# Attention in front of two MoE layers: where in two passes the next pair of heads' bias is read

## The chip, the cores and the metric

The kernel runs on one NeuronCore of one Trainium2 chip. The metric is the device time of one launch in microseconds. Three runs of the kernel before took 1263.3, 1264.17 and 1265.56 us; the median is 1264.17 us. The change and every reading of the trace here are about that one core.

## The reference

The program is an attention layer followed by a dense MoE layer and a second MoE layer whose gate is balanced by row and column sums. Only the attention matters for the change:

```python
B, H, S, D = 2, 8, 576, 64
scores = scale * np.matmul(q, k.transpose(0, 1, 3, 2))
psi_rel = np.log1p(np.abs(rel))
x = (psi_rel / psi_i)[..., None]
h = np.maximum(x @ w1 + b1, 0.0)
bias = h @ w2
scores = scores + bias.transpose(2, 0, 1)[None, :, :, :]
attn = np.exp(scores - max); attn = attn / (sum + 1e-09)
out = np.matmul(attn, v)
...
```

The bias belongs to a head and a pair of positions, and not to a batch: both batches add the same bias.

## The kernel before, in words

The kernel has three stages. First `bias_emit` builds the bias of all heads and writes it to five tensors in HBM, `wt0` to `wt4`, one for each of the five blocks of query rows (four of 128 rows, one of 64). Then `attention` (L350) runs. Last come the two MoE layers, set up in `experts` and started by `rest`.

Heads go in pairs, so there are four pairs, and each pair has two passes, one per batch: pass i works on pair i // 2 and on batch i % 2. A pass has nine steps, one for each of `TILES` (L57), which names the block of query rows t and the head o of the pair. Block 1 and block 0 come first, then 3, 4 and 2. The step number r within a pass places all side work by hand, and s = 9 i + r counts the steps over all eight passes. `soft` (L377, its instruction is at L386) adds the bias to the scores in PSUM on DVE and takes the minimum; ACT then takes the exponential, POOL or ACT the division, PE the transposes and the product with v.

The side work that the prediction follows:

- `read(hp, t)` (L1136) reads block t of pair hp's bias from HBM into a tile that has two buffers, so pair hp + 1 writes the buffer that pair hp - 1 has left. Blocks 0 to 3 are one DMA each (L1147). Block 4 is three DMAs (L1149 to L1151). All are issued on SyncE's queue (SP).
- `load` (L296) brings q (`qr`, L306), k (`kr`, L306) or v (L300) of a pass to SBUF, q and k as two DMAs each. q and k share one buffer, `raw`, so k of a pass can only be loaded when q of that pass has been used up, and q of the pass after that only when k has.
- `prep(i, k)` (L308) cuts q and k into a high and a low part: DVE copies the high part (L282, `qh` or `ks`), POOL subtracts (L321 `ql`, L332 `ks`). By `PREPS` (L59), pass i's steps 0 and 4 do this for pass i + 1: at step 0 the parts of q, and behind them the load of k for pass i + 1; at step 4 the parts of k, and behind them the load of q for pass i + 2. `VLOAD` puts the load of v at step 2.
- `beside` (L993) places early work of the MoE by `EARLY` (L72). Six of its weight loads (L581) stand at s = 10, 12, 30, 34, 42 and 48, and DVE and POOL convert the loaded weights in four parts; the first part of the first piece (L590, DVE) stands at s = 14, which is step 5 of pass 1.

What sets the order: SP issues its DMAs strictly in the order in which the program emits them, and each waits only for its own buffers and sources. The step at which a read is emitted thus fixes only its place among SP's other issues. Each compute engine works through its own instructions in order as well.

Of the kernel before, what the change touches and what calls it, by code (L numbers as in the profile page):

```python
# [19 lines left out]
HP = H // 2  # L20
# [39 lines left out]
VLOAD = 2  # L60
COPIES = "ddd"
NORM = "apppapppa"
PVLAST = (9, 7, 5, 0, 0)
EPSLAST = "pdd"
EPS = "ddppddddp"
# [25 lines left out]
def attention_moe_moe_kernel(ctx: ExitStack, tc, qT, kT, vN, wpos, w_in, w_out, w_gate, e_w1, e_w2,  # L91
# [258 lines left out]
    def attention(sp, pre, biases, read, xr, beside, ep):  # L350
# [7 lines left out]
        def qk(i, t, o):  # L358
            st = state[i]
            b, hp = pairs[i]  # L360
            sps = ps2("sps")
            qh, ql, ks = st["qh"], st["ql"], st["ks"]
            if t == 4:
                ops = [(z[:, 64 * h:64 * h + 128], h) for h in range(2) for z in st["z"]]
            else:
                ops = [(x[:, o, 128 * t:128 * t + 128], o) for x in (qh, ql)]
            for k, (lhs, h) in enumerate(ops):
                if t == 4 and h == 1:
                    spans = [(0, 0, 288, 64), (1, 0, 224, 352), (1, 224, 288, 0)]
                else:  # L370
                    spans = [(0, 0, 288, 0), (1, 0, 288, 288)]
                for hf, c0, c1, k0 in spans:
                    nc.tensor.matmul(sps[:, hf, c0:c1], lhs, ks[:, h, k0:k0 + c1 - c0],  # L373
                                     start=(k == 0), stop=(k == len(ops) - 1 and c1 == 288))
            st["s", t, o] = sps

        def soft(i, t, o):  # L377
            st = state[i]
            b, hp = pairs[i]
            sps = st["s", t, o]  # L380
            if o == 0:
                st["p", t] = sp.tile([128, 2 * S], F32, tag="p", bufs=4, name="p")
                st["sm", t] = sp.tile([128, 8], F32, tag="sm", bufs=4, name="sm")
            p, sm = st["p", t][:, S * o:S * o + S], st["sm", t]
            bias = biases[hp, t] if t == 4 else biases[hp, t][:, :, o]
            nc.vector.tensor_tensor_reduce(  # L386
                out=p.rearrange("p (a j) -> p a j", a=2), in0=sps[:, :, 0:288],
                in1=bias.rearrange("p (a j) -> p a j", a=2),
                scale=-0.125, scalar=3.0e38, op0=ALU.add, op1=ALU.min, accum_out=sm[:, o:o + 1])
            nc.scalar.activation(p, p, AF.Exp, bias=sm[:, o:o + 1], scale=-1.0, accum_out=sm[:, 2 + o:3 + o])  # L390

        def norm(i, t, o, r):
# [3 lines left out]
            nc.vector.reciprocal(sm[:, 6 + o:7 + o], sm[:, 4 + o:5 + o])  # L396
            if NORM[r] == "a":
                nc.scalar.activation(p, p, AF.Copy, scale=sm[:, 6 + o:7 + o])
# [13 lines left out]
        def transp(i, t, o):  # L412
            st = state[i]
            ch = 0 if t < 2 else 1
            if ("pt", ch) not in st:
                st["pt", ch] = [sp.tile([128, 4, 320], F32R, tag=f"pt{x}", bufs=2, name="pt") for x in range(2)]
                st["po", ch] = sp.tile([128, 5, 320], F32, tag="po", bufs=2, name="po")
                st["tps", ch] = ps.tile([128, 512], F32, tag="tail", bufs=1, name="tps")
            (hi, lo), odd = st["pt", ch], st["po", ch]
            p = st["p", t]  # L420
            tp = ps.tile([128, 4, 128], F32, tag="t", bufs=2, name="tp")
            k0 = (S + 64) * o
            for kt in range(4):
                nc.tensor.transpose(tp[:, kt], p[:, k0 + 128 * kt:k0 + 128 * kt + 128], ident)  # L424
            tps = st["tps", ch]
            c0 = 128 * t - QOFF[ch]
            if t != 4:
                c = slice(c0, c0 + 128)
                if o == 1:
                    nc.tensor.transpose(tps[:, c], p[:, 512:640], ident)  # L430
                    copy(tp, odd[:, 0:4, c], ODD[r_now[0]])
                else:
                    evac(tp, hi[:, :, c], lo[:, :, c])
            else:

                nc.tensor.transpose(tps[:, c0 - 64:c0 + 64], p[:, 448:576], ident)
                nc.tensor.transpose(tps[0:64, c0:c0 + 128], p[:, 512:576], ident)
                c = slice(c0, c0 + 64)
                evac(tp[:, :, 0:64], hi[:, :, c], lo[:, :, c])
                copy(tp[:, :, 64:128], odd[:, 0:4, c], ODD[r_now[0]])  # L440
            if t in (1, 3) and o == 1:
                n = QLEN[ch]
                copy(tps[:, 0:n], odd[:, 4, 0:n], TAIL[ch])

        def pv(i, ch, part):


            st = state[i]
            b, hp = pairs[i]
            n = QLEN[ch]  # L450
            vh, vl = st["v"]
            if part == 0:
                st["op", ch] = ps.tile([128, 512], F32, tag="pv", bufs=1, name="op")
            op = st["op", ch]
            if part < 4:
                rh, rl = (x[:, part, 0:n] for x in st["pt", ch])
                trips = [(vh[:, part], rh), (vh[:, part], rl), (vl[:, part], rh)]
            else:
                trips = [(st["vr"][:, 256 + 128 * (part - 4):384 + 128 * (part - 4)], st["po", ch][:, part - 4, 0:n])]
            for k, (l, r) in enumerate(trips):  # L460
                nc.tensor.matmul(op[:, 0:n], l, r, start=(part == 0 and k == 0), stop=(part == 8))  # L461
            part = 3 if part == 8 else 0
            if part == 3:
                a, z = b * S + QOFF[ch], b * S + QOFF[ch] + n
                while a < z:
                    e = min(z, (a // CH + 1) * CH)
                    xs = (xr[a // CH][:, hp, a % CH:a % CH + e - a], op[:, n - (z - a):n - (z - e)])
                    tails.append(lambda xs=xs: nc.scalar.activation(xs[0], xs[1], AF.Copy))
                    a = e
# [8 lines left out]
        for s in range(len(pairs) * NT + 5):  # L478
            if s >= 5:
                total = min(total + PVS[s % NT], len(parts))  # L480
            at.append(total)
        for n, k in enumerate(PVLAST):
            at[n - len(PVLAST)] = len(parts) - k
        seq = [(i, t, o) for i in range(len(pairs)) for t, o in tiles]
        lows, tails = [], []
        qk(*seq[0])
        for s in range(len(seq) + LAG + 2):
            i, r = divmod(s, NT)
            r_now[0] = r
            for w in ORDER[r]:  # L490
                if w == "t" and 0 <= s - LAG < len(seq):
                    transp(*seq[s - LAG])
                elif w == "q" and s + 1 < len(seq):
                    qk(*seq[s + 1])
                elif w == "p":
                    for n in range(at[s - 1] if s else 0, at[s]):
                        pv(*parts[n])
            if LOWFIRST[r]:
                for f in lows:
                    f()  # L500
                lows.clear()
            if s < len(seq):
                soft(*seq[s])
            for f in tails + lows:
                f()
            tails.clear()
            lows.clear()
            if 0 <= s - 1 < len(seq):
                norm(*seq[s - 1], (r - 1) % NT)
            if s == 2:  # L510
                prep(0, 5, sp)
            for k, at_r in enumerate(PREPS):
                if at_r == r:
                    prep(i + 1, k, sp)
            if r == VLOAD and i + 1 < len(pairs):
                load(i + 1, "v", sp)
            if r < 5 and i % 2 == 1 and i // 2 + 1 < HP:
                read(i // 2 + 1, (0, 1, 4, 2, 3)[r])
            beside(s, ep)


# [602 lines left out]
    with tc.manual_schedule(), ExitStack() as stack:  # L1124
# [11 lines left out]
        def read(hp, t, eng=nc.sync):  # L1136


            n = 128 if t < 4 else 64
            biases[hp, t] = dst = bp.tile([128, S, 2] if t < 4 else [128, S], F32, tag=f"bias{t}", bufs=2, name="bias")  # L1140
            src = wt[t][:]

            def keys(row, c, j0, j1):
                return bass.AP(tensor=src.tensor, offset=src.offset + row * c * WROW + c * (n - 1 + j0),
                               ap=[[H * WROW - c, n], [1, c * (j1 - j0)]])
            if t < 4:
                eng.dma_start(out=dst.rearrange("p s o -> p (s o)"), in_=keys(hp, 2, 0, S))  # L1147
            else:
                eng.dma_start(out=dst[0:64], in_=keys(hp, 1, 0, S))  # L1149
                eng.dma_start(out=dst[64:128, 0:512], in_=keys(HP + hp, 1, 64, S))  # L1150
                eng.dma_start(out=dst[64:128, 512:S], in_=keys(HP + hp, 1, 0, 64))  # L1151
# [76 lines left out]
```

## Time and profile before

| what | before |
|---|---|
| median of three runs | 1264.17 us |
| the profiled execution's own time | 1263.23 us |
| its span | 1261.4 us |
| PE busy | 1195.8 us, 95% |
| DVE busy | 828.9 us, 66% |
| ACT busy | 492.7 us, 39% |
| POOL busy | 571.9 us, 45% |
| TensorE's granted clock, mean | 0.989 of full speed |
| DMA queue of SP | 89.35 MB, 23.4% of 16 engines' span |

The span runs from the first to the last instruction; the profiled execution's own time is 1.8 us longer, and 0.9 us under the median. Busy shares are means over the whole span, in which the attention's eight passes take about 170 us (105 to 275 us) and the MoE layers nearly all the rest. So what bounds the attention has to be read from its own stretch.

### The profile page before, as it was taken

The numbers are of one execution on the slowest core, as the hardware profiler recorded it, in microseconds if no ns is written. First come the engines' busy times: TensorE is split into PE (matmuls) and PEld (weight loads), VectorE is DVE, ScalarE is ACT, GpSimd is POOL, SyncE is SP. The second block draws the span as 40 slices with busy tenths as digits, with TensorE's granted clock in tenths as the row PEclk, the third lists the DMA queues.
The fourth block names the chain that finished last, engine by engine and source line by source line (L and its number), as shares of the span: only waits on it lengthen the run. The fifth ranks groups of instructions, "written<-read, shape, count | busy, mean of one in ns | idle before, by whom it ended". The sixth has DMA issues, their size and how long they took to land.

```text
span 1261.4 us, 19043 instructions
## 1 busy us (share of the span) xinstructions
PE 1195.8 (95%) x7460; PEld 1004.5 (80%) x7460; DVE 828.9 (66%) x1489; ACT 492.7 (39%) x861; POOL 571.9 (45%) x445
## 2 busy tenths in 40 slices
PE   5777799999999999999999999999999999999998
PEld 4777687887887886777888888888888888888887
DVE  8985678755777767367566566666665665665665
ACT  7865566675322334432432232232232332232321
POOL 1124577656444555353344444444444454453440
PEclk9889999999999999999999999999999999999999
DMA  3576645603222311111111111111111111111102
GB/s 98 156 209 173 173 141 149 187 1 101 84 85 74 109 52 46 38 40 45 34 51 50 34 51 50 34 51 51 35 50 50 42 43 51 50 36 49 34 1 76
DMA packets 58573, 90.86 MB, mean 72 GB/s; under 512 B 6900, under 2 KB 37236, under 8 KB 58484
## 3 DMA queue, kind: packets, MB, share of 16 engines
q1 hardware_dynamic: 58196, 89.35, 23.4%
q8 instruction: 58, 0.95, 0.3%
q10 hardware_dynamic: 288, 0.30, 0.1%
q14 instruction: 31, 0.25, 0.1%
HBM read 74.45 MB, written 15.19 MB: 71 GB/s over the span
## 4 chain that ended last, share of the span: by engine, by line
PE 79%; DVE 11%; DMA 4%; POOL 2%; issue 2%; ACT 1%; SPq 0%; POOLq 0%; DVEq 0%
PE sum L783 33%; PE t L688 16%; PE pv L797 4%; PE tail L756 3%; PE tail L688 3%; PE pv L688 3%; PE t L703 3%; DMA raw<-in_qT_dram 3%; PE op L461 2%; PE pac L201 2%; DVE m L191 2%; PE pv L703 2%; PE tail L703 2%; PE sps L373 1%; PE tp L424 1%
## 5 line engine op out<-in xcount | busy, mean ns | idle before, releaser
L626 POOL TENSOR_TENSOR wu<-f,wu 128x1024 fp32r<-128x1024 f32 x72 | 172.7, 2399 | 439.5 <-ACT wu L625 439.0
L783 PE MATMUL sum<-wd,h 128*128 128x512 f32 x1536 | 365.3, 393 | 0.0
L783 PEld LDWEIGHTS sum<-wd,h 128*128 128x128 f32 x1536 | 283.2, 188 | 56.4
L816 DVE SCALAR_TENSOR_TENSOR acc<-sum,prob,acc 128x512 f32<-128x512 f32 x224 | 168.2, 751 | 137.6 <-PE sum L783 137.6
L688 PE MATMUL t<-room,wu 128*128 128x512 f32 x512 | 142.5, 390 | 0.0
L688 PE MATMUL t<-x,wu 128*128 128x512 f32 x448 | 123.9, 392 | 3.0 <-ACT x L667 1.6
L626 POOL TENSOR_TENSOR wd<-f,wd 128x1024 fp32r<-128x1024 f32 x40 | 96.1, 2402 | 36.8 <-ACT wd L625 29.2
L688 PEld LDWEIGHTS t<-room,wu 128*128 128x128 f32 x512 | 96.3, 188 | 19.9
L738 ACT ACTIVATE v<-t 128x512 f32<-128x512 f32 x32 | 19.1, 597 | 233.3 <-PE t L688 233.3
L688 PEld LDWEIGHTS t<-x,wu 128*128 128x128 f32 x448 | 84.5, 189 | 22.3 <-POOL x L649 2.1
L201 PE MATMUL pac<-bw,m 128*128 128x64 bf16 (+1 forms) x1920 | 69.6, 201 | 33.2 <-DVE extra L225 15.1
L783 PE MATMUL sum<-h,wd 128*128 128x512 f32 x384 | 93.9, 397 | 1.7 <-DVE acc L814 1.2
L201 PEld LDWEIGHTS <-m 128*128 128x128 bf16 (+1 forms) x1920 | 66.5, 107 | 36.2 <-issue 26.5
L783 PEld LDWEIGHTS sum<-h,wd 128*128 128x128 f32 x384 | 69.9, 188 | 20.4 <-DVE acc L814 5.9
L625 ACT ACTIVATE wu<-f 128x1024 fp32r<-128x1024 f32 x72 | 75.8, 1053 | 15.3 <-DVE f L607 15.3
L591 POOL TENSOR_SCALAR f<-f 128x512 f32<-128x512 f32 x32 | 61.8, 1939 | 30.0 <-DVE f L590 29.7
L814 DVE TENSOR_TENSOR acc<-sum,acc 128x512 f32<-128x512 f32 x80 | 55.0, 688 | 23.7 <-PE sum L783 23.0
L390 ACT ACTIVATE p<-p,sm 128x576 f32<-128x576 f32 x72 | 55.6, 773 | 28.1 <-DVE sm L386 14.5
L707 DVE TENSOR_TENSOR tail<-tail,v 128x512 f32<-128x512 f32 x32 | 22.4, 699 | 66.3 <-PE tail L688 66.3
L723 ACT ACTIVATE hl<-tail 128x256 fp32r<-128x256 f32 x40 | 15.3, 383 | 127.1 <-PE tail L765 127.1
L723 ACT ACTIVATE h<-pv 128x512 fp32r<-128x512 f32 x40 | 23.9, 599 | 99.1 <-DVE pv L707 98.9
L625 ACT ACTIVATE wd<-f 128x1024 fp32r<-128x1024 f32 x40 | 42.4, 1060 | 47.3 <-DVE f L607 47.3
(192 smaller groups left out, 2171.8 us busy)
## 6 DMA issues: line engine op xcount, KB each, us to landing
f<-in_e_w_dram SPq DMA_DIRECT2D x128, 256.0 KB, 2.9
bias<-wt SPq DMA_DIRECT2D x16, 576.0 KB, 6.5
raw<-in_w_in_dram SPq DMA_DIRECT2D x16, 512.0 KB, 3.6
raw<-in_w_out_dram SPq DMA_DIRECT2D x16, 512.0 KB, 3.6
wt<-extra SPq DMA_DIRECT2D x10, 512.0 KB, 4.3
raw<-in_qT_dram SPq DMA_DIRECT2D x16, 288.0 KB, 6.8
raw<-in_kT_dram SPq DMA_DIRECT2D x16, 288.0 KB, 4.4
vr<-in_vN_dram SPq DMA_DIRECT2D x8, 448.0 KB, 6.6
```

The lines of the kernel that those rows point to most:

```text
L201: nc.tensor.matmul(pt[0:n, g], lhs, win(w, (k * (ng + 1) + gw) * NC, [[(ng - gw) * NC, 2], [1, NC]]), start=(k == 0), stop=(k == 2))
L390: nc.scalar.activation(p, p, AF.Exp, bias=sm[:, o:o + 1], scale=-1.0, accum_out=sm[:, 2 + o:3 + o])
L591: nc.gpsimd.tensor_scalar(t, t, F64_MIN, F64_MAX, ALU.max, ALU.min)
L625: nc.scalar.activation(w[:, 0], src, AF.Copy)
L626: nc.gpsimd.tensor_tensor(out=w[:, 1], in0=src, in1=w[:, 0].bitcast(F32), op=ALU.subtract)
L688: nc.tensor.matmul(z[n], wu(u)[:, a, o:o + 128], xs[xn][b][j], start=(k == 0), stop=(k == 5))
L703: nc.tensor.matmul(zz, wu(u)[:, a, o:o + 128], xs[f"A{c + 1}{k // 2 + 1}"][b][k % 2], start=(k == 0 and n == 0), stop=(k == 3 and n == 2))
L723: nc.scalar.activation(t[:, 0], src, AF.Copy if u < U1 else AF.Relu)
L783: nc.tensor.matmul(s, lhs, rhs, start=(n == 0), stop=(n == 5))
L797: nc.tensor.matmul(r, t[:, b, 128 * f:128 * f + 128], w[:, a, f], start=(n == 0), stop=(n == 5))
L814: nc.vector.tensor_tensor(out=d, in0=o, in1=d, op=ALU.add)
L816: nc.vector.scalar_tensor_tensor(out=d, in0=o, scalar=pool["prob"][:, t, e:e + 1], in1=d, op0=ALU.mult, op1=ALU.add)
```

## The change

The five reads of the next pair's bias stood in the first five steps of a pair's second pass, in the order of blocks 0, 1, 4, 2, 3. Now a table gives each its pass of the pair and its step: block 0 at step 6 and block 1 at step 8 of the first pass, block 4 at step 1, block 2 at step 3 and block 3 at step 6 of the second.

```diff
+AHEAD = {(0, 6): 0, (0, 8): 1, (1, 1): 4, (1, 3): 2, (1, 6): 3}
...
             if r == VLOAD and i + 1 < len(pairs):
                 load(i + 1, "v", sp)
-            if r < 5 and i % 2 == 1 and i // 2 + 1 < HP:
-                read(i // 2 + 1, (0, 1, 4, 2, 3)[r])
+            if i // 2 + 1 < HP and (i % 2, r) in AHEAD:
+                read(i // 2 + 1, AHEAD[i % 2, r])
             beside(s, ep)
```

Within a step the order of emission is: `prep`, the load of v, the read, `beside`.

## Rows read from the trace of the kernel before

**Rows 1.** The page's first part: span, and PE's busy time, share, instructions.

```profile
span 1261.4 us, 19043 instructions
PE 1195.8 (95%) x7460; PEld 1004.5 (80%) x7460; DVE 828.9 (66%) x1489; ACT 492.7 (39%) x861; POOL 571.9 (45%) x445
```

**Rows 2.** Stretches: passes 1, 2, 7, the rest; length, busy, PEclk, DMA share, GB/s.

```profile
123.65:147.85 24.20, 20.31 (x127) 17.81 (x127) 14.75 (x48) 14.55 (x34) 15.11 (x19) 0.93 0.72 195
147.85:173.84 25.99, 21.63 (x137) 18.89 (x136) 19.36 (x51) 14.39 (x34) 14.97 (x15) 0.93 0.35 89
...
256.62:274.90 18.28, 18.27 (x128) 16.62 (x127) 12.58 (x41) 16.06 (x38) 8.96 (x13) 1.00 0.00 1
284.00:1261.40 977.40, 966.97 (x4504) 796.55 (x4503) 616.74 (x972) 293.68 (x465) 435.87 (x277) 1.00 0.16 51
```

**Rows 3.** DVE in order of time: start, duration, instruction, [idle before <-releaser].

```profile
125.78 0.76 DVE L282 CAST qh<-raw 128x1152 fp32r<-128x1152 f32 x1 [0.60 <-DMA raw<-in_qT_dram]
...
140.55 0.43 DVE L590 TENSOR_SCALAR f<-raw 128x512 int32<-128x512 int32 x1 [4.50 <-DMA raw<-in_w_in_dram]
...
151.97 0.76 DVE L282 CAST qh<-raw 128x1152 fp32r<-128x1152 f32 x1 [2.29 <-DMA raw<-in_qT_dram]
...
196.10 0.76 DVE L282 CAST qh<-raw 128x1152 fp32r<-128x1152 f32 x1 [1.30 <-DMA raw<-in_qT_dram]
...
240.01 0.76 DVE L282 CAST qh<-raw 128x1152 fp32r<-128x1152 f32 x1 [1.80 <-DMA raw<-in_qT_dram]
```

**Rows 4.** The chain that ended last, attention's stretch: start, length, what it was.

```profile
120.18 5.51 DMA raw<-in_qT_dram
...
140.54 11.34 DMA raw<-in_qT_dram
...
189.33 6.68 DMA raw<-in_qT_dram
...
230.83 9.09 DMA raw<-in_qT_dram
```

**Rows 5.** SP's issues in order of time in pass 1: start, duration, DMA.

```profile
129.51 1.11 SPq L306 DMA_DIRECT2D raw<-in_kT_dram  x2
130.66 1.06 SPq L1147 DMA_DIRECT2D bias<-wt  x2
131.76 0.43 SPq L581 DMA_DIRECT2D raw<-in_w_in_dram  x1
...
138.62 2.41 SPq L306 DMA_DIRECT2D raw<-in_qT_dram  x2
```

**Rows 6.** The page's sixth part, DMA issues: count, KB each, us to landing.

```profile
bias<-wt SPq DMA_DIRECT2D x16, 576.0 KB, 6.5
```

**Rows 7.** Landing of pass 1's k load (L306), then of the two reads behind it (L1147).

```profile
L306 SPq DMA_DIRECT2D raw<-in_kT_dram x2: 465/530/596, 129.5 to 130.0; - x2
DMA to landing us min/median/max: 4.2/4.2/4.2
...
L1147 SPq DMA_DIRECT2D bias<-wt x2: 432/508/584, 130.7 to 131.3; - x2
DMA to landing us min/median/max: 6.4/6.8/7.2
```

**Rows 8.** Short stretches of the attention; columns as in rows 2.

```profile
122.00:130.00 8.00, 7.91 (x55) 7.05 (x54) 7.30 (x24) 6.58 (x15) 5.62 (x7) 1.00 0.16 38
130.00:152.00 22.00, 18.20 (x116) 16.27 (x114) 10.63 (x36) 11.73 (x28) 10.93 (x15) 0.92 0.91 243
138.00:144.00 6.00, 2.19 (x14) 1.51 (x12) 2.83 (x11) 2.30 (x6) 3.32 (x5) 1.00 1.04 272
144.00:148.00 4.00, 4.00 (x18) 3.60 (x19) 2.38 (x10) 1.25 (x3) 2.60 (x4) 0.57 1.08 240
...
156.00:162.00 6.00, 4.02 (x12) 2.90 (x13) 4.26 (x12) 2.22 (x5) 3.00 (x4) 0.72 0.64 175
...
240.00:244.00 4.00, 2.79 (x19) 2.21 (x18) 3.92 (x12) 2.46 (x6) 2.97 (x3) 1.00 0.01 5
```

## The prediction, made before the kernel was run

> **What bounds the kernel now.** The page's first part comes first: PE is busy for 95% of the span [rows 1]. That is a mean over two very different stages. The table by stretches parts them: behind 284 us PE works 966.97 of 977.40 us, so the MoE layers are bound by PE, and a microsecond gained ahead of them is a microsecond of the whole. The attention is not so: its last pass, with the DMA engines at rest, takes 18.28 us with PE busy throughout, while passes 1 and 2 take 24.20 and 25.99 us [rows 2]. What the slow passes wait for is in DVE's timeline: DVE stood still 4.50 us for a weight load (L590, pass 1), and 2.29, 1.30 and 1.80 us for q (L282, step 0 of passes 2, 4 and 6), each time for a DMA [rows 3]. The chain that ended last runs through the same three loads of q, 11.34, 6.68 and 9.09 us long; the one issued in pass 0 took 5.51 us [rows 4]. All three late loads are issued in a pair's second pass, the one that holds the five bias reads. SP's order shows why they are late: in pass 1 the load of k is followed at once by two bias reads, and only then come the weight load for which DVE waits and, further back, q [rows 5]. The DMA engines are 0.91 busy from 130 to 152 us, moving 243 GB/s, and 0.16 busy in the 8 us before [rows 8]. So the queue of transfers is the bound there.
>
> **What the change does, part by part.** SP knows no steps, only an order. Reads 0 and 1 stood right behind the load of k in the second pass; now they stand right behind the load of q of the first pass (q is emitted at step 4, nothing else of SP's lies between it and step 6; in pass 4 a weight load without a near user comes between the two reads). Their emission at steps 6 and 8 therefore does not delay them: I expect both to go out as soon as q is issued. Read 4 moves ahead of v and of the weight load at s = 10. Read 2 keeps its place ahead of its weight load, and read 3, though two steps later, is still the first issue behind q. No instruction is added or removed; per pair two transfers leave the crowded pass, and this happens for three pairs.
>
> Term 1, pass 1. A read is 576 KB [rows 6], two are 1.18 MB. The second half of k was issued at 130.0 and landed 4.2 us later, at 134.2; the two reads behind it had landed by 137.7 at the earliest and 138.5 at the latest reading [rows 7]. So they held the queue for 3.5 to 4.3 us; I take 4.0. Bounds: nothing, if what follows only goes slower; above, 1.18 MB at the crowded mean of 243 GB/s, 4.85 us [rows 8]. Against that, read 4 (half a read, 288 KB) now stands ahead of the weights: 4.0 x 288 / 1152 = 1.0 us. The weights land near 140.55 - 4.0 + 1.0 = 137.55. DVE was ready at 140.55 - 4.50 = 136.05 [rows 3], so 1.5 us of wait remain and 3.0 are gained. q has the same transfers ahead of it as before but for the two reads, so it lands at 151.97 - 4.0 = 147.97. DVE reaches it at 149.68 - 3.0 = 146.68 and waits 1.3 us. Together the gain of passes 1 and 2 is what q gains, **4.0 us**; what is late next is still q, and behind it the converts of pass 2.
>
> The Trainium skill (HBM Reference, Specifications) states about 425 GB/s for a core that streams alone, against the 243 that the crowded stretch shows. By it the two reads would hold the queue an estimated 2.8 us, and the sum below would be 5.3 us. The measured rate decides, since these are the same transfers in the same company.
>
> Term 2, pass 4. The late q was issued from 189.33 and took 6.68 us, to 196.0 [rows 4]. Taken 4.0 earlier the queue would let it land at 192.0; alone it needs at least the 4.2 us that k's half needed [rows 7], so 193.5. DVE was ready at 194.8 [rows 3]. The whole 1.30 us goes: **1.3 us** (bounds 0 and 1.3).
>
> Term 3, pass 6. q ended at 239.92 [rows 4] and would end near 235.9; DVE was ready at 238.21. The wait of 1.80 goes, but here PE soon paces: from 240 to 244 it works 2.79 of 4.00 us [rows 8], so it can give back 1.21. **1.2 us** (bounds 0 and 1.8).
>
> Edits costed at nothing. Reads 0 and 1 in the first pass: cover is the idle queue (0.16 busy, 122 to 130) [rows 8]; 4.0 us behind q's landing at 125.7 [rows 4] ends at 129.7, as k is issued at 129.51 [rows 5]. Without that cover k would be late by up to 4.85 us, and DVE's copy at step 4 with it. Waits: read 0 needs its buffer, left by the pair before the present one, and SP holds k of the next pass behind it; those users are a full pass older, so no wait. Arrival: the reads come earlier or at the same place in the order, their first use is in the next pair. SP's own time is equal, as the issues are.
>
> Sum: 4.0 + 1.3 + 1.2 = 6.5 us. Against the profiled execution's 1263.23 us this is 1256.7; the median is 0.9 us above that execution, so 1264.17 - 6.5 = **1257.7 us**.
>
> **The rivals.** A: the stalls move on and the gain is mostly given back, because the emptied place in the queue is taken by slower transfers. For it: the rate falls from 272 to 240 GB/s as the burst goes on [rows 8], so what comes behind the reads is slower than they are. Against it: q of pass 1 has the same company behind the reads in both kernels. With a third of term 1, 1.2 us, and half of the others, 0.6 and 0.6, it is 2.4 us: 1261.8 us.
>
> B: more than the sum. In pass 1 PE works 2.19 of 6 us (138 to 144), and then has a granted clock of 0.57 for 4 us, 1.2 GHz for most of it; the clock falls again around 156 to 162 (0.72 over 6 us), behind the wait for q [rows 8]. Each fall loses about 1.7 us of PE time ((1 - 0.57) x 4 and (1 - 0.72) x 6). In the first, q paces pass 2 anyway, so I count nothing for it in the sum; if PE enters pass 2 ahead and one fall goes in full, 1.7 us come on top: 1256.0, with both 1254.3. The Trainium skill (TensorE: Matmul & The Clock Gate, The HAM clock gate) states that an array left idle drops to 1.2 GHz and that activity releases it, by which a shorter wait would spare the fall. The trace agrees in so far as both falls follow idle PE.
>
> C: slower. The reads behind q are not behind it in effect: q's rows and theirs are moved side by side, and q of the first pass lands late, up to 4.85 us for each of three pairs. In pass 1 this counts in full, DVE already waits 0.60 us for that q [rows 3]; in passes 3 and 5, where DVE shows no such wait, half: 4.85 + 2.4 + 2.4 = 9.7, less 6.5, is 3.2 slower, 1267.4 us. It decides from a delay of some 9 us in all, where it outweighs the gain by what can be measured. Against it: k of pass 1 landed in 4.2 us with the two reads right behind it [rows 7].
>
> That the change does not do what it says is partly so: reads spread over steps are no spread on SP, and read 3 does not move at all. Only two of five count.
>
> **How the numbers follow.** The forecast has 0.50, B 0.20, A 0.19, C 0.11. A difference of 0.2% (2.5 us) is about what a measurement of this kernel can tell from none; the three runs shown spread over 0.18%. Forecast and B are faster, 0.70, and a little of A falls beyond the bound: faster 0.72, same 0.18, slower 0.10. The range goes from below B with both falls gone, 1253.2, to A with nothing gained, 1264: it leaves out C and a little of B.
>
> **What the changed profile would show.** In SP's timeline two bias reads right behind q in passes 0, 2 and 4, and read 4 behind k. In DVE's, the wait at L590 near 1.5 us, that for q in pass 2 near 1.3, none in passes 4 and 6, and no new wait for q in passes 1, 3 and 5 beyond the 0.60. Passes 1 and 2 together about 46 us. Wrong would be: late q or k in the odd passes (C), or equal DVE waits with other releasers, POOL's or PE's, in passes 2 and 4 (A).

## The result, and the profile after

Four runs of the changed kernel have a median of 1254.35 us (1252.02 to 1255.79), four of the kernel before 1264.79 us. The ratio is 0.992 with an interval of 0.990 to 0.994: faster by 0.8%, some 10 us, where 6.5 us and 1257.7 us were forecast. The time lies in the stated range (1253.2 to 1264.0), nearest to rival B's figures.

The profiled execution took 1255.24 us, 8.0 less than the one before. Its first part, against [rows 1]:

```profile
span 1253.5 us, 19043 instructions
PE 1194.6 (95%) x7460; PEld 1005.2 (80%) x7460; DVE 830.0 (66%) x1489; ACT 493.2 (39%) x861; POOL 572.8 (46%) x445
```

Busy times are nearly the same over the whole span; what went is idle time. The table by stretches says where. The rows are passes 1 to 7, each from DVE's first addition of bias to the next pass's first, and the rest of the span; columns as in [rows 2].

```profile
122.84:142.79 19.95, 18.17 (x128) 16.56 (x127) 16.00 (x47) 14.50 (x34) 14.32 (x17) 1.00 0.85 263
142.79:165.82 23.03, 20.24 (x137) 18.05 (x136) 19.07 (x50) 14.38 (x34) 16.00 (x17) 1.00 0.34 90
165.82:185.07 19.25, 17.67 (x123) 16.02 (x122) 14.11 (x45) 15.07 (x35) 14.84 (x18) 1.00 0.68 207
185.07:206.64 21.57, 19.62 (x134) 17.30 (x133) 18.85 (x51) 14.45 (x34) 17.61 (x19) 1.00 0.53 159
206.64:228.53 21.89, 19.92 (x125) 17.56 (x124) 15.79 (x47) 15.09 (x34) 16.35 (x19) 0.93 0.67 211
228.53:247.45 18.92, 18.92 (x133) 17.50 (x132) 14.01 (x45) 14.33 (x33) 11.08 (x14) 0.99 0.20 57
247.45:265.73 18.28, 18.27 (x128) 16.62 (x127) 12.58 (x41) 16.10 (x39) 9.02 (x13) 1.00 0.00 1
275.00:1253.50 978.50, 966.54 (x4503) 796.57 (x4502) 616.86 (x972) 294.12 (x465) 436.21 (x277) 1.00 0.16 51
```

The same cuts of the kernel before, those that [rows 2] leaves out:

```profile
173.84:193.07 19.23, 17.65 (x123) 16.01 (x122) 14.10 (x46) 15.05 (x35) 14.78 (x18) 1.00 0.68 216
193.07:216.01 22.94, 19.97 (x134) 17.34 (x133) 18.95 (x51) 14.44 (x34) 17.56 (x19) 1.00 0.51 147
216.01:236.48 20.47, 18.55 (x126) 16.44 (x125) 15.78 (x47) 15.09 (x34) 15.46 (x18) 1.00 0.71 200
236.48:256.62 20.14, 18.93 (x132) 17.21 (x131) 14.03 (x45) 14.29 (x33) 11.89 (x16) 1.00 0.35 91
```

In these two traces passes 1 and 2 took 50.19 us together and now take 42.98: 7.2 gained. Pass 4 gained 1.4 (a second trace of each kernel, further down, shares the gain out otherwise). Passes 5 and 6 together lost 0.2 (40.61 to 40.81), passes 3 and 7 are equal. With 0.8 us that pass 1 already began earlier, the attention ends 9.2 us sooner (DVE's last addition of bias at 263.63 in place of 272.82). Of that the MoE part lost 1.3 again, which leaves the 7.9 us between the spans.

DVE's timeline answers to [rows 3]. These are the same kind of instructions, at the first weight piece and at the copies of q in step 0 of passes 1, 2, 4 and 6. A bracket is the idle time before an instruction, with what ended it; a copy without a bracket did not wait:

```profile
124.31 0.74 DVE L284 CAST qh<-raw 128x1152 fp32r<-128x1152 f32 x1
135.63 1.52 DVE L592 TENSOR_SCALAR f<-raw 128x512 int32<-128x512 int32 x1 [0.80 <-DMA raw<-in_w_in_dram]
144.53 0.74 DVE L284 CAST qh<-raw 128x1152 fp32r<-128x1152 f32 x1
186.72 0.74 DVE L284 CAST qh<-raw 128x1152 fp32r<-128x1152 f32 x1
230.43 0.74 DVE L284 CAST qh<-raw 128x1152 fp32r<-128x1152 f32 x1
```

The brackets are gone from every q, and the wait at the weights fell from 4.50 to 0.80 us. Before, that wait and the three for q in passes 2, 4 and 6 came to 9.9 us; 9.1 of them are gone. SP's order in the changed kernel, against [rows 5]:

```profile
118.85 1.11 SPq L308 DMA_DIRECT2D raw<-in_qT_dram  x2
120.01 1.06 SPq L1149 DMA_DIRECT2D bias<-wt  x2
128.05 1.11 SPq L308 DMA_DIRECT2D raw<-in_kT_dram  x2
129.21 0.60 SPq L1151 DMA_DIRECT2D bias<-wt  x1
...
131.12 0.59 SPq L583 DMA_DIRECT2D raw<-in_w_in_dram  x1
...
136.89 1.12 SPq L308 DMA_DIRECT2D raw<-in_qT_dram  x2
```

Reads 0 and 1 go out at 120.01, right behind q, though the program puts them at steps 6 and 8. The two halves of pass 1's q, issued from 136.89, no longer stand in a queue: the landing that the trace records came 4.2 us after the issue, against 11.9 before. The DMA engines' work and the granted clock in the stretches that answer to [rows 8]:

```profile
136.00:142.00 6.00, 4.22 (x31) 3.78 (x29) 5.36 (x16) 3.85 (x10) 5.72 (x7) 1.00 1.04 321
142.00:146.00 4.00, 4.00 (x32) 3.87 (x31) 3.49 (x12) 3.26 (x8) 1.71 (x4) 1.00 0.23 89
148.00:154.00 6.00, 3.93 (x22) 3.02 (x21) 4.72 (x11) 2.79 (x6) 3.23 (x3) 1.00 0.66 172
224.00:228.00 4.00, 3.26 (x14) 2.89 (x15) 1.73 (x7) 1.14 (x3) 2.98 (x5) 0.67 0.66 209
492.00:517.00 25.00, 22.53 (x109) 16.85 (x110) 6.32 (x14) 9.88 (x17) 11.58 (x9) 0.93 0.13 43
```

The burst is over by 146 us in place of 152. Both falls of the granted clock in passes 1 and 2 are gone, and with them PE's busy time in the two passes fell from 41.9 to 38.4 us for the same work, 3.5 of the 7.2 us. A fall has come in pass 5, at 224 us, and the MoE's start ran at 0.93 where the kernel before had 0.95 in the like stretch (500 to 525 us).

### The profile page after: what moved, and what is told of

Same layout as the page of the kernel before. It is cut to its first block, busy times and chain, and to the rows that moved or that the text cites. A ratio compares the mean times of both kernels' runs of the same rounds, so it can differ in the third digit from the quotient of the medians.

```text
span 1253.5 us, 19043 instructions
## 1 busy us (share of the span) xinstructions
PE 1194.6 (95%) x7460; PEld 1005.2 (80%) x7460; DVE 830.0 (66%) x1489; ACT 493.2 (39%) x861; POOL 572.8 (46%) x445
## 4 chain that ended last, share of the span: by engine, by line
PE 81%; DVE 11%; POOL 3%; issue 2%; ACT 1%; DMA 1%; SPq 0%; POOLq 0%; DVEq 0%
PE sum L785 33%; PE t L690 17%; PE pv L799 4%; PE tail L758 3%; PE pv L690 3%; PE tail L690 3%; PE t L705 3%; PE op L463 3%; PE pac L203 2%; PE sps L375 2%; PE tp L426 2%; DVE m L193 2%; PE pv L705 2%; PE tail L705 2%; DVE f L598 1%
## 5 line engine op out<-in xcount | busy, mean ns | idle before, releaser
L740 ACT ACTIVATE v<-t 128x512 f32<-128x512 f32 x32 | 19.2, 600 | 233.1 <-PE t L690 233.1
L709 DVE TENSOR_TENSOR tail<-tail,v 128x512 f32<-128x512 f32 x32 | 22.4, 699 | 66.2 <-PE tail L690 66.2
```

## The experiments

Theory Q: a load is late by what stands in front of it in SP's order, whatever it is; steps play no part. Its rivals: S, the spread itself matters; T, the total load of the second pass matters; R, the bias reads are special. After the first runs theory P was added: read 4's place changes the burst's rate. Ratios are to the kernel before on the same chip, with their interval in brackets. Each run left one trace, so a time has a spread behind it and a wait has none. In all sketches below `AHEAD` is the table of the change, {(pass of the pair, step): block}.

**Only reads 0 and 1.**

```diff
-AHEAD = {(0, 6): 0, (0, 8): 1, (1, 1): 4, (1, 3): 2, (1, 6): 3}
+AHEAD = {(0, 6): 0, (0, 8): 1, (1, 2): 4, (1, 3): 2, (1, 4): 3}
```

> Only reads 0 and 1 move to the first pass; reads 4, 2 and 3 keep the places they had before (steps 2, 3 and 4 of the second pass). Theory Q (what stands in front of q and of the first weight piece in SP's order is what counts, and of the change only the two moved reads matter): the whole gain, 1252.5 to 1256.5 us, no wait for q in passes 2, 4 and 6, and the wait at the first weight piece (0.80 us with the change) gone or near it, since half a read less stands in front. Rival S (the spread itself matters: read 4 ahead of the weights and read 3 two steps later carry a good part): 1258 to 1261 us.

Measured: 1254.68 us, ratio 0.9938 (0.9924 to 0.9951). The time is Q's, but not the waits:

```profile
136.65 0.46 DVE L592 TENSOR_SCALAR f<-raw 128x512 int32<-128x512 int32 x1 [1.85 <-DMA raw<-in_w_in_dram]
...
146.29 0.76 DVE L284 CAST qh<-raw 128x1152 fp32r<-128x1152 f32 x1 [1.72 <-DMA raw<-in_qT_dram]
```

The weights have 288 KB less in front of them than with the change, and come later here: DVE takes them up 8.6 us after k's first issue, against 7.6. That is this trace's; the run with the two reads left out, further down, has the same order in pass 1, and there they landed 6.8 us after k (issued at 127.64, 5.6 us to landing, k at 126.49), as byte counting has it. Of the change's 7.2 us in passes 1 and 2 this kernel has 4.8 (19.94 + 25.49 us). Pass 1 is as short as with the change; pass 2 is not, with its wait for q and a clock of 0.93:

```profile
142.75:168.24 25.49, 21.71 (x137) 19.23 (x136) 19.36 (x51) 14.38 (x34) 15.93 (x17) 0.93 0.38 104
```

**All five behind q, in the second pass.**

```diff
+AHEAD = {(1, 4): 1, (1, 5): 0, (1, 6): 3, (1, 7): 4, (1, 8): 2}
```

> All five reads stay in the second pass, but behind the load of q (steps 4 to 8, blocks 1, 0, 3, 4, 2), so the pass moves as many bytes as before. Theory Q: no wait for q or for the weights, so nearly the gain of the change; against it the bias of blocks 1 and 0 lands late for step 0 of the next pass, by 1 to 2 us for each of three pairs: 1255 to 1260 us, with waits of DVE for bias in its place. Rival T (what counts is how much the second pass transfers in all): no gain, 1263 to 1266 us.

Measured: 1258.89 us, 0.9970 (0.9956 to 0.9985). As Q expects, no wait for q or the weights is left in the second passes although they move as many bytes; T, which expected no gain, falls. The price is there too, but once, not three times:

```profile
188.74 0.76 DVE L388 CUSTOM_DVE_ANT_0 p<-sps,bias 128x576 f32<-128x576 f32 x1 [2.57 <-DMA bias<-wt]
```

**The same order at other steps.**

```diff
+AHEAD = {(0, 4): 0, (0, 5): 1, (1, 1): 4, (1, 3): 2, (1, 4): 3}
```

> Reads 0 and 1 at steps 4 and 5 of the first pass in place of 6 and 8, read 3 at step 4 of the second in place of 6. SP's order is that of the changed kernel but for one swap (read 1 ahead of a weight load in pass 4). Theory Q: the changed kernel's time, 1252 to 1257 us, with reads 0 and 1 issued right behind q as there. Rival S (the steps hold the reads back): other issue times, and a time over 1257 us.

Measured: 1253.32 us, 0.9929 (0.9914 to 0.9943), the changed kernel's time within the intervals; reads 0 and 1 leave right behind q (120.19 us, q from 119.04). The steps do not count, SP's order does.

**All five in the first pass.**

```diff
+AHEAD = {(0, 4): 0, (0, 5): 1, (0, 6): 3, (0, 7): 4, (0, 8): 2}
```

> All five reads in the first pass, behind its load of q (blocks 0, 1, 3, 4, 2). Theory Q: 2.65 MB now stand in front of k of the second pass; at 243 to 300 GB/s they hold the queue 9 to 11 us behind q, so k lands 2 to 4 us late and DVE waits that long for it at step 4 of passes 1, 3 and 5: 1258 to 1264 us. Rival T (the emptier the second pass the better): 1251 to 1254 us, no new wait for k.

Measured: 1260.47 us, 0.9983 (0.9970 to 0.9995). Q again, more sharply in pass 1 than expected, not at all in pass 3: k is the late one, as five reads outlast the quiet stretch.

```profile
140.57 0.76 DVE L284 CAST ks<-raw 128x1152 fp32r<-128x1152 f32 x1 [7.27 <-DMA raw<-in_kT_dram]
228.26 0.76 DVE L284 CAST ks<-raw 128x1152 fp32r<-128x1152 f32 x1 [3.83 <-DMA raw<-in_kT_dram]
```

**Other bytes out of the burst.** The kernel before, with two weight pieces loaded a pass earlier.

```diff
-EARLY = ((10, 14, 16, 19), (12, 20, 22, 25),
+EARLY = ((6, 14, 16, 19), (8, 20, 22, 25),
```

> The kernel before, all five reads where they were, but the first two weight pieces (1.05 MB) are loaded at steps 6 and 8 of pass 0 in place of steps 1 and 3 of pass 1. Theory Q (bytes in front of what is waited for, whatever they are): the wait of 4.5 us at the first weight piece goes, q of pass 1 is no longer late or by under 1 us, so passes 1 and 2 gain 5 to 7 us; the waits for q in passes 4 and 6 stay at 1.3 and 1.8: 1257 to 1260 us. Rival R (the bias reads themselves are what makes the burst slow): q in pass 2 still waits 2 us or more, 1260 to 1263 us.

Measured: 1260.43 us, 0.9974 (0.9960 to 0.9989).

```profile
147.65 0.76 DVE L282 CAST qh<-raw 128x1152 fp32r<-128x1152 f32 x1 [2.43 <-DMA raw<-in_qT_dram]
191.68 0.76 DVE L282 CAST qh<-raw 128x1152 fp32r<-128x1152 f32 x1 [1.12 <-DMA raw<-in_qT_dram]
236.01 0.76 DVE L282 CAST qh<-raw 128x1152 fp32r<-128x1152 f32 x1 [2.09 <-DMA raw<-in_qT_dram]
```

The time and the 2.43 us are R's, yet R's reason finds no support. From k's first issue to the end of the wait for q it is 147.65 - 128.28 = 19.4 us, against 151.97 - 129.51 = 22.5 before: 1.05 MB of weights gave 3.1 us. The two reads alone (1.18 MB) gave 4.2 (146.29 - 128.01 = 18.3). Against the second trace of the kernel before, further down, both would be at least 1.4 us less; the bias reads are not shown to weigh more per byte than the weights. My number for Q was wrong: with the weights' wait gone DVE is ready for q about 3 us earlier after k's issue (16.9 us against 20.2), so most of the wait for q returns. Passes 4 and 6 kept their waits, as expected.

**The two reads left out.** Reads 0 and 1 of pairs 1 to 3 are not made at all.

```diff
+            if hp and t < 2:
+                biases[hp, t] = biases[0, t]
+                return
```

> The kernel before with reads 0 and 1 of pairs 1 to 3 left out (those pairs use pair 0's bias for blocks 0 and 1), reads 4, 2 and 3 where they were. It prices the two reads. Theory Q (in the first pass they cost nothing): the time of the run in which only these two move, 1253 to 1256.5 us, and the same wait for q in pass 2, 1.7 us. Rival (the moved reads still cost something behind q): 1250 to 1252.5 us.

Measured: 1253.64 us, 0.9922 (0.9902 to 0.9942), the time of the kernels in which these reads move. In their new place they cost nothing that can be measured. The wait of 1.7 us for q in pass 2 that I expected did not come, though SP's order in pass 1 is that of the run with 1.72 us: two bursts of one order differ by some 2 us. Without the wait pass 2 is as short as with the change, at a clock of 1.00:

```profile
141.84:164.86 23.02, 20.24 (x137) 18.06 (x136) 19.07 (x51) 14.39 (x34) 15.93 (x17) 1.00 0.31 82
```

Passes 1 and 2 together take 43.56 us, against 42.98 with the change and 45.43 in the run that moves only these two reads.

**Read 4 first, nothing leaves the pass.**

```diff
-                read(i // 2 + 1, (0, 1, 4, 2, 3)[r])
+                read(i // 2 + 1, (4, 0, 1, 2, 3)[r])
```

> The kernel before with read 4 first among the five reads of the second pass (order 4, 0, 1, 2, 3 at steps 0 to 4): nothing leaves the pass. Theory P (transfers of 64 partitions slow all that moves with them; with read 4's three right behind k, itself of 64 partitions, the rest of the burst runs at over 350 GB/s): q of pass 1 lands 3 to 5 us earlier than before, its waits in passes 2, 4 and 6 shrink, 1257 to 1261 us. Theory Q alone (bytes in front): q has the same bytes in front of it, the weights 0.3 MB less, so 1262 to 1265 us, and q as late as before.

Measured: 1258.76 us, 0.9960 (0.9946 to 0.9974), which is P's time, and a gain by order alone. q ends 146.36 - 127.02 = 19.3 us after k's first issue, 3.2 earlier than in the first trace of the kernel before, at the lower end of P's 3 to 5, and at most 1.7 earlier than in the second. The wait for q in pass 4 is 3.44 us; the kernel before has 1.30 and 5.02 there in its two traces. The edit does two things, though: it also puts read 1 behind the first weight piece and v, and the wait at the weights is 3.14 us in place of 4.50.

**Read 4 as one transfer to 128 partitions, and its smallest part first.** Both start from the run with only reads 0 and 1 moved.

```diff
+                if hp:
+                    w0 = wt[0][:]
+                    eng.dma_start(out=dst, in_=bass.AP(tensor=w0.tensor, offset=w0.offset + hp * 2 * WROW + 254,
+                                                       ap=[[H * WROW - 2, 128], [1, S]]))
+                    return
```

> As the run in which only reads 0 and 1 move (read 4 behind v), but read 4 of pairs 1 to 3 is one transfer to 128 partitions with as many bytes (from another bias tensor, so block 4 of those pairs gets other numbers) in place of three to 64 partitions each. Theory P (transfers to 64 partitions slow what moves among them): from the first issue of k to the landing of q pass 1 takes 13 to 15 us, as with the change, and not 18.1, and DVE has no wait for q in pass 2. Theory O (only the place of the bytes in SP's order counts, not their shape): 17.5 to 18.5 us and a wait of 1.5 to 2 us. The whole run 1251 to 1255 us by P, 1253 to 1256 by O.

Measured: 1256.11 us, 0.9920 (0.9895 to 0.9946); no wait for q in any pass.

```diff
-                read(i // 2 + 1, AHEAD[i % 2, r])
+                t = AHEAD[i % 2, r]
+                read(i // 2 + 1, t, piece=0 if t == 4 else None)
+            if i // 2 + 1 < HP and (i % 2, r) == (1, 1):
+                read(i // 2 + 1, 4, piece=1)
```

Here piece 1 is the 16 KB transfer and piece 0 the two large ones.

> As the run in which only reads 0 and 1 move, but of read 4's three transfers the smallest (16 KB, rows of 256 bytes) goes out right behind k, ahead of the first weight piece; the two large ones stay behind v. Theory P: 64 partitions are what slows, so pass 1 still takes 17 to 18.5 us from k's issue to q's landing, with DVE waiting 1 to 2 us for q in pass 2. Rival K (the small rows in the middle of the burst slow it): 13.5 to 15 us and no wait.

Measured: 1255.43 us, 0.9912 (0.9883 to 0.9941); no wait for q either. By the expectation P falls with that, since the two large transfers to 64 partitions still stood among the rest; but the run with the two reads left out had no wait either, with read 4 unsplit behind v, so one trace without a wait cannot decide for or against P, O or K. A measure that does not hang on when DVE is ready is when the second weight piece lands, counted from k's first issue. The rows, for the kernel before, the run with only two reads moved, and the changed kernel (SP's issue; landing in us after it):

```profile
L581 SPq DMA_DIRECT2D raw<-in_w_in_dram x1: 385/385/385, 137.1 to 137.1; - x1
DMA to landing us min/median/max: 11.6/11.6/11.6
```

```profile
L583 SPq DMA_DIRECT2D raw<-in_w_in_dram x1: 610/610/610, 133.4 to 133.4; - x1
DMA to landing us min/median/max: 10.6/10.6/10.6
```

```profile
L583 SPq DMA_DIRECT2D raw<-in_w_in_dram x1: 433/433/433, 132.7 to 132.7; - x1
DMA to landing us min/median/max: 7.0/7.0/7.0
```

| kernel | reads 0, 1 in the burst | read 4 | second weight piece landed, us after k |
|---|---|---|---|
| before | yes | behind v | 137.1 + 11.6 - 129.5 = 19.2 |
| before, second trace | yes | behind v | 18.4 |
| read 4 first | yes | first | 16.8 |
| only two moved | no | behind v | 16.0 |
| two left out | no | behind v | 13.9 |
| 16 KB part first | no | split | 13.4 |
| read 4 in one | no | behind v, 128 partitions | 11.7 |
| changed | no | first | 132.7 + 7.0 - 128.0 = 11.7 |
| changed, second trace | no | first | 11.7 |
| other steps | no | first | 12.3 |

On the means, taking the two reads out is worth 18.8 - 15.0 = 3.8 us and read 4's place another 15.0 - 11.9 = 3.1. Every kernel of the lower seven rows moves the same bytes up to there, so the second is a difference of order; with single traces that differ by 2.1 us in one order, its size lies anywhere between 1.6 (13.9 - 12.3) and 4.3 us (16.0 - 11.7). Why the three transfers of read 4 cost as much in the middle of the burst, their 64 partitions, the 256-byte rows of the smallest, or what they meet, the runs do not settle. Nor do the times show the 3.1 us: the run that moves only two reads (0.9938) and the changed kernel (0.992 and 0.9911) overlap in their intervals.

**The changed kernel and the kernel before once more.**

> The changed kernel once more, for its spread and for a second trace. If the granted clock's fall in pass 5 (0.67 over 224 to 228 us) and the 1.3 us that the MoE's start lost are chance, they are gone or elsewhere in this trace and the end of the attention differs by 1 to 2 us: 1252 to 1256 us. If they belong to the change, both return in the same place and size.

Measured: 1252.60 us, 0.9911 (0.9892 to 0.9931). Passes 2, 5 and 6, and the MoE's start:

```profile
142.19:165.91 23.72, 21.25 (x137) 18.94 (x136) 19.32 (x51) 14.38 (x34) 15.95 (x17) 0.93 0.32 90
206.68:227.26 20.58, 18.55 (x126) 16.45 (x125) 15.79 (x48) 15.09 (x34) 15.57 (x18) 1.00 0.76 233
227.26:245.39 18.13, 18.13 (x130) 17.02 (x129) 14.02 (x44) 14.31 (x33) 11.91 (x16) 1.00 0.22 61
489.00:514.00 25.00, 23.84 (x119) 17.46 (x118) 7.29 (x15) 10.50 (x18) 12.54 (x9) 0.95 0.14 43
```

The fall of pass 5 is gone, another stands in pass 2, and the MoE lost nothing: the attention ended 11.2 us before the old one, the span is 1250.1 us, 11.3 less. So the falls' places change from trace to trace of one kernel. Even equal idle time of PE does not fix them. These are the same 4 us of pass 2 in the changed kernel's two traces, the first trace on top; PE is busy for 2.05 us in both:

```profile
148.60:152.60 4.00, 2.05 (x9) 1.57 (x10) 3.96 (x11) 1.76 (x4) 1.24 (x3) 1.00 0.67 159
148.00:152.00 4.00, 2.05 (x4) 1.46 (x5) 3.96 (x11) 1.76 (x4) 1.24 (x3) 0.75 0.65 175
```

> The kernel before once more, for a second trace. If pass 1's burst is the same each time, q lands 22 to 23 us after k's first issue again, with the waits of 4.5 and 2.3 us on DVE behind it. If it was chance, 18 to 21 us and smaller waits.

Measured: 1262.71 us, one run. The burst is somewhat shorter: q had landed by 21.0 us after k's first issue at the latest (DVE copies it at 148.37 without a wait, k from 127.33), where 22 to 23 us would have meant the same burst each time. The waits share out otherwise: 4.47 us at the weights, none at q in pass 2, and

```profile
195.69 0.76 DVE L282 CAST qh<-raw 128x1152 fp32r<-128x1152 f32 x1 [5.02 <-DMA raw<-in_qT_dram]
239.68 0.76 DVE L282 CAST qh<-raw 128x1152 fp32r<-128x1152 f32 x1 [1.55 <-DMA raw<-in_qT_dram]
```

Their sum is 11.0 us, against 9.9 in the first trace, and its last addition of bias came at 272.42 (272.82). Where a wait falls is loose; what the late transfers cost in all is not. Passes 1, 2 and 4 of this trace:

```profile
122.12:146.19 24.07, 20.45 (x128) 18.17 (x127) 14.86 (x48) 14.38 (x34) 15.16 (x19) 0.88 0.75 212
146.19:169.68 23.49, 20.83 (x137) 18.65 (x136) 19.10 (x50) 14.39 (x34) 15.03 (x15) 0.98 0.30 81
188.92:215.91 26.99, 21.24 (x134) 18.33 (x133) 18.95 (x51) 14.46 (x34) 17.59 (x19) 0.94 0.56 142
```

So passes 1 and 2 take 47.56 us here and 50.19 in the first trace, pass 4 26.99 and 22.94. The changed kernel's second trace has 43.68 for passes 1 and 2 and 21.55 for pass 4. By the second traces the change gives 3.9 us in passes 1 and 2 and 5.4 in pass 4, by the first ones 7.2 and 1.4; the sum of the three passes is steadier, 9.3 and 8.6.

**Three reads behind q.**

```diff
+AHEAD = {(0, 6): 0, (0, 8): 1, (1, 5): 3, (1, 6): 4, (1, 7): 2}
```

> Reads 0 and 1 in the first pass as with the change; reads 3, 4 and 2 all behind the load of q in the second (steps 5, 6 and 7). Theory Q: nothing but k, v and the weights stands in front of q, so the wait of 0.8 us at the first weight piece goes too and no new wait comes, as blocks 3, 4 and 2 are used from step 4 of the next pair on: 1250.5 to 1254 us, at best 0.8 us under the changed kernel in the trace. Rival: three reads in front of the next k make it late, 1255 to 1258 us.

Measured: 1254.15 us, 0.9905 (0.9879 to 0.9932). The wait at the weights is gone, and no new wait for a DMA comes; in time it cannot be told from the change. Yet its going bought nothing: pass 1 is 2.3 us longer than the change's 19.95.

```profile
122.35:144.63 22.28, 19.84 (x128) 17.98 (x127) 15.34 (x47) 14.27 (x34) 15.51 (x19) 0.92 0.75 224
```

The clock falls in it, to 0.92 in the mean, and PE waits 2.4 us for a division on POOL, against 1.8 with the change. Where k was not late, pass 1 took 20.3 to 22.4 us in all six kernels with no more than 0.15 us of wait at the weights, and 19.9 to 20.0 in the four traces with 0.7 to 1.9 us of it. Why, the runs do not settle.

## Why the prediction was right, and where its sum was short

**Right: the bound and the mechanism.** The queue of transfers ahead of q and the weights was the bound, two reads leaving it were the gain, and SP's order, not the step, decides. The run with the reads left out, the one at other steps and the one behind q each show a part of it.

**Right on the means: the price of the two reads.** 4.0 us of queue were forecast; 3.8 is the difference of the means in the table, with single pairs of traces from 2.4 to 5.3. The measured rate of the burst gave this, not the 425 GB/s of the Trainium skill (HBM Reference, Specifications), by which it would have been an estimated 2.8.

**Too small: terms 1 and 2.** Together they forecast 5.3 us for passes 1, 2 and 4; the two pairs of traces show 8.6 and 9.3. Three steps of the working were mis-sized.

- "q has the same transfers ahead of it as before but for the two reads, so it lands at 151.97 - 4.0 = 147.97." The bytes were the same, the time was not. With the change q landed 4.2 us after its issue, as soon as k's half had, and was not waited for at all in place of 1.3; the weights' wait was 0.80 and 0.73 in place of 1.5. The run that leaves read 4 behind v came nearer to the working, with 1.85 us at the weights, 1.72 at q and 45.4 us for the two passes, where 46 were foretold; the changed kernel took 43.0 and 43.7. How much of the difference is read 4's place and how much one burst's chance stays open: the run with the two reads left out, with the same order there, had no wait and 43.6.
- The fall of the clock behind the wait in pass 1, for which the sum counts nothing. Pass 1 ran at 0.93 and 0.88 before and at 1.00 in both traces of the change, and PE's busy time in it fell from 20.3 and 20.5 to 18.2 us. How much of that would have been gained with q still late, no run separates.
- The waits were taken from one trace as if they were fixed. Term 2's 1.3 us agree with the first traces' 1.4 by luck of that pair: the second trace of the kernel before waited 5.02 us at the same place, and there the change gave 5.4.

**About right, cap too tight: term 3.** The changed kernel's first trace shows -0.2 for passes 5 and 6, since the clock fell in pass 5. Its second, without that fall, shows 40.61 - 38.71 = 1.9, all of the wait of 1.80. My cap, PE's 1.21 us of idle time in four microseconds, was too tight.

**The edits at nothing.** Held: DVE's wait for k in pass 1 is 0.69 us, and was 0.79 before; no bias comes late. The cover that I named is real, as the run with five reads in the first pass shows, where k is 7.27 us late.

**The rivals.** A fell for the changed kernel: the waits are gone and no others took their place. (In A's working a third of 4.0 is 1.3 and not 1.2, which moves its time by 0.1 us.) C fell: q of pass 1 lost even its 0.60 us, which the second trace of the kernel before does not have either. B is in part seen, and nearer to the time than the forecast was. In the first trace both falls that it names are gone. In pass 2 a fall is worth less than the 1.7 us of my working: with one, in the second trace, the pass is 0.7 us longer (23.72 against 23.03). In pass 5 it is 1.3 (21.89 against 20.58). How much of the gain beyond the sum is B's and how much is that of q coming sooner the runs do not part.

## What to carry to other kernels

Where transfers share one in-order queue, look at what stands in front of the load that an engine waits for, and not at the step where the program puts it: moving two reads past q in the order gave the gain, moving reads by steps nothing. Put prefetches behind the last urgent load of a quiet stretch, and no more of them than that stretch holds. When a burst bounds, its order can count as well as its bytes, so a sum of bytes over a mean rate may give only part of the gain. Before pricing a change by single waits, take a second trace of the kernel before: here a wait was 1.30 us in one and 5.02 in the other, and only the sum over the passes held.

## What the runs showed that I had not expected

A burst's duration varies, and the place of one small read seems to move it: with the same bytes the second weight piece landed 11.7 to 16.0 us after k's first issue. The three traces with read 4 first lie within 0.6 us of one another, while another order gave 16.0 and 13.9. The granted clock's falls move from trace to trace of the same kernel (224 us in one, 148 to 156 in the other); in one stretch the clock was 1.00 in one trace and 0.75 in the other, with PE busy for 2.05 of 4 us in both. The changed kernel's two traces differ by 3.4 us in span: 2.0 of it by the end of the attention, the rest at the MoE's start. And a DMA wait that is taken away need not be a gain: without the wait at the weights pass 1 was longer than with a short one.
